# Block sums of two head pairs turned in one product, token rows stored ahead of their gate weights, and seven steps at other places of a hand-written order

## The chip, the core and the metric

The kernel runs on one core of one Trainium2 chip. The engines named here are TensorE (PE; its weight loads are PEld in the trace), VectorE (DVE), ScalarE (ACT), GpSimd (POOL) and SyncE (SP, which issues most transfers). The metric is the device time of one execution in microseconds, as the median of several runs.

## The reference

Local-plus-summary attention, and a mixture of experts on its output, cut to what matters:

```python
k_sum = k.reshape(B, H, nb, block, D).max(axis=3)      # B=2, H=8, S=768, D=64, block=32, nb=24
v_sum = v.reshape(B, H, nb, block, D).mean(axis=3)
scores_all = concat([where(|i-j| < 16, scale*q@k.T, -1e9), scale*q@k_sum.T + log(block)])
x = (softmax(scores_all) @ concat([v, v_sum])).reshape(1536, 512)
logits = x @ w_gate;  expert = argmax(logits);  gate_w = max softmax(logits)     # 8 experts
h = relu(x_of_expert @ w1[e]);  y = h @ w2[e];  out[token] = gate_w * y          # capacity 384
```

## The kernel before, in words

**Attention.** Two heads are worked on together; there are eight such pairs c = 0 to 7, four per batch. Each pair has three groups of four query tiles, so 24 groups n. A group has five steps, whose names stand in the order list: S (scores, PE, L284), M (row maxima, DVE, L291), E (exponentials, four ACT instructions, L295), R (turn, four PE transposes, L299) and K (copy of the turned block, ACT, L304). `V` with a pair and a half (V00, V01, ..., V71) is the product with the values (PE, L310), `N` its normalization (DVE, two steps, L321). Scores lie in two PSUM buffers that alternate (in the first half of the list in three), probabilities in two, so S of a group waits for E of two groups before.

**Keys and values of a pair.** `k`, `q`, `t`, `v` with a number are the loads (SP). `w` copies key windows, `kb` takes block maxima on DVE, `kp` copies them behind the windows (its letter p, v or a is the engine: POOL, DVE or ACT). `vb` sums the values over blocks on DVE into `vsq` (L262), `vt` turns these sums with one PE transpose into a corner of the PSUM tile `bank` (L266), `vk` copies the corner to `vrow` (ACT, L269), `vp` and `vP` copy `vrow` under the value windows (POOL, L272). `bank` also holds the gate logits and the token lists, and a PE product into it waits for an ACT copy out of it that stands ahead in the order list.

**Routing.** For each batch r, `x` turns token rows (PE), `X` copies them, `l`/`L`/`g` make the gate logits, `ch` chooses experts, `pf` makes prefix sums, `pl` places tokens (its last steps write `colm`, L430), `ga` makes the gate weight and stores the rows of the batch to `xrow` in DRAM (L443). `tk0` (PE, L459) makes the token lists of batch 0, `rows` (DVE) the row numbers of the first expert's tokens, `fr0` to `fr2` (POOL) fetch those rows indirectly.

**Experts.** Three rounds, their names without a letter, with B and with C. `lw`/`lW` load w1 and w2 in four parts, `h1g` rounds part g of w1 (or `h2g` of w2) to its high part, `s1g` (and `s2g`) takes the low part as a difference; a letter at the end is the engine (`s10v`: low part of w1, part 0, on DVE, L584). `T`, `H`, `I` turn a third of the fetched rows (PE), round it (ACT) and take its low part `xl` (DVE). `u0` to `u7` are the up products (PE, L629: high by high, low by high, high by low), `D` the down products (L646).

**What sets the order.** The list `SEQ` (L113) is written by hand; each name in it records its instructions at once, and every engine executes its own instructions in that order. An instruction at the head of its engine's row that waits holds all behind it. SP's transfers go through one hardware queue, and each also waits for an earlier use of one of eight completion semaphores.

Of the kernel before, what the change touches and what calls it, by code (L numbers as in the profile page):

```python
# [110 lines left out]


SEQ = """  # L113
q1 k1 t0 S0 k2 t2 S1 M0 E0 M1 Q11a q2 Q10p w1p q3 kb1 S2 E1 kp1v R0 M2 S3 E2 vb0 R1 z2 z3 t1 K0 K1 k3 v0 Q20p w2p vt0 M3 kb2 v2 vk0 S4 vb2 kp2p E3 v1
R2 Q21a M4 S5 q4 K2 t3 E4 Q30p vP0 k4 R3 M5 Q31a vp0 S6 vb1 E5 misc t4 R4 M6 w3p q6 S7 K3 kb3 v3 E6 vt1 M7 V00 kp3p q5 vk1 K4 V01 vp1 N00 N00 vP1 R5
N01 N01 E7 S8 K5 R6 M8 S9 K6 E8 R7 M9 vt2 vk2 V10 E9 vP2 V11 N10 N10 Q41a Q40p S10 N11 N11 K7 vp2 k5 vb3 R8 S11 M10 t5 K8 w4p kb4 E10 R9 M11 vt3 kp4p
V20 vk3 K9 vP3 V21 N20 E11 vb4 S12 vp3 N21 t6 N20 Q60p k6 Q61a N21 R10 M12 k7 R11 K10 S13 E12 vt4 K11 M13 V30 vk4 V31 E13 Q50p N30 N30 S14 N31 Q51a
N31 w5p kb5 R12 x0 M14 K12 kp5p x1 vb5 X0a x2 X1a S15 t7 vb6 X2a q7 E14 v6 vt5 M15 l00 w6p vk5 kb6 v5 R13 L00a E15 R14 w7p v4 kb7 x3 g00 K13 v7 S16
X3a kp6p vb7 K14 vP4 x4 M16 x5 Q70p X4a S17 X5a vp4 Q71a vt6 kp7p E16 M17 l01 vp5 R15 vP5 L01a E17 S18 vk6 g01 K15 M18 vp6 R16 ch0 S19 vP6 E18 ch0 ch0
ch0 ch0 R17 ch0 ch0 M19 S20 ch0 ga0 E19 ga0 ga0 pf0 ga0 pick pick pick M20 pick pick pick pick first lw0 lw1 lw2 lw3 V40 pl0 K16 pl0 V41 N40 pl0 K17  # L120
N40 S21 N41 N41 pl0 pl0 pl0 R18 pl0 pl0 E20 R19 vt7 vk7 vP7 vp7 zr V50 pl0 pl0 pl0 pl0 K18 M21 V51 K19 N50 N50 E21 tk0 rows rows S22 N51 N51 ts0 pads
pads R20 pads M22 rows fr0 S23 K20 pads E22 pads pads pads firstB R21 fr1 M23 K21 V60 E23 V61 fr2 N60 N60 h10a R22 N61 N61 R23 K22 s10v V70 K23 V71
lW0 lW1 lwB0 h11p h12p h13p N70 N70 x6 x7 X6a x8 X7v N71 N71 T0 X8a T1 H0 l10 I0 H1 I1 L10a T2 x9 H2 x10 I2 g10 X9v X10a x11 u0 X11a s11v l11 L11a
# [12 lines left out]
def attention_moe(ctx: ExitStack, tc: tile.TileContext, qT, kT, vT, vw, wg, w1, w2, cf, cm, cr, cv, out, cap: int):  # L136
    nc = tc.nc
# [12 lines left out]
    xrow = dram.tile([N, XW], F32, name="xrow")  # L150
# [179 lines left out]
    class Route:  # L330
# [22 lines left out]
        def take(self, i, eng):  # L353
            self.xt[i] = work.tile([P, KD, P], F32, tag="xt", name="xt", bufs=LB)
            cast(eng, self.xt[i], self.xp[i])

        def logits(self, j):
            self.lq[j] = psum.tile([P, LB, P], F32, tag="x" if self.n == 0 else f"av{j}", name="lq", bufs=1)
            for i in range(LB):
                for kk in range(KD):  # L360
                    nc.tensor.matmul(self.lq[j][32 * kk : 32 * kk + 32, i, :], wgt[:, kk, :], self.xt[LB * j + i][:, kk, :], start=True, stop=True)

        def logits_keep(self, j, eng):
            self.lqs[j] = work.tile([P, LB, P], F32, tag="lqs", name="lqs", bufs=1)
# [82 lines left out]

    def clip(cn, name):
# [525 lines left out]
```

## Time and profile before

| what | value |
|---|---|
| median of 3 runs (lowest, highest) | 188.87 us (188.63, 191.33) |
| the profiled execution's own time | 189.09 us |
| its span, first to last instruction | 187.0 us |
| what lies around the span | 2.09 us |
| PE busy, PEld busy | 174.2 us (93%), 156.2 us (84%) |
| DVE, ACT, POOL busy | 104.7, 101.3, 67.3 us |
| mean granted TensorE clock | 0.992 |

The span falls into two parts. Up to about 75 us attention and routing run, with all engines at work; from there to about 180 us the three expert rounds run, and PE works through nearly without a gap. A busy PE row counts matmuls that overlap, so gaps are read from the weight loads (PEld): idle time ahead of one, and what ended it, is a real stop of PE. A row of the timeline is start, duration, engine, line, operation, output and inputs, shapes, count, and in brackets the idle time before it and what ended that.

### The profile page before, as it was taken

The numbers are of one execution on the slowest core, as the hardware profiler recorded it, in microseconds if no ns is written. First come the engines' busy times: TensorE is split into PE (matmuls) and PEld (weight loads), VectorE is DVE, ScalarE is ACT, GpSimd is POOL, SyncE is SP. The second block draws the span as 40 slices with busy tenths as digits, with TensorE's granted clock in tenths as the row PEclk, the third lists the DMA queues.
The fourth block names the chain that finished last, engine by engine and source line by source line (L and its number), as shares of the span: only waits on it lengthen the run. The fifth ranks groups of instructions, "written<-read, shape, count | busy, mean of one in ns | idle before, by whom it ended". The sixth has DMA issues, their size and how long they took to land. (4 is left out here: it accounts for less than half of the span.)

```text
span 187.0 us, 3978 instructions
## 1 busy us (share of the span) xinstructions
PE 174.2 (93%) x1461; PEld 156.2 (84%) x1461; DVE 104.7 (56%) x226; ACT 101.3 (54%) x223; POOL 67.3 (36%) x84
## 2 busy tenths in 40 slices
PE   6969999999898979999999999999999999999950
PEld 2858899999698968999987889999888999988830
DVE  3499668695389876469998476455611932210000
ACT  4679999998875757346455375445324722211110
POOL 7399758566614599200072341200022110002220
PEclk9999999999999999999999999999999999999996
DMA  6989999939949995277999999970011010001011
GB/s 188 332 318 307 272 365 312 378 93 295 270 147 285 354 404 176 81 255 266 259 407 319 351 389 401 413 294 4 0 56 55 1 60 0 2 4 56 29 38 58
DMA packets 20375, 38.77 MB, mean 207 GB/s; under 512 B 1482, under 2 KB 8572, under 8 KB 20348
## 3 DMA queue, kind: packets, MB, share of 16 engines
q1 hardware_dynamic: 18416, 33.43, 54.2%
q0 software_dynamic: 1440, 4.73, 6.3%
q10 hardware_dynamic: 492, 0.28, 0.6%
q8 instruction: 13, 0.21, 0.5%
q14 instruction: 14, 0.11, 0.2%
HBM read 29.77 MB, written 8.66 MB: 206 GB/s over the span
## 5 line engine op out<-in xcount | busy, mean ns | idle before, releaser
L646 PE MATMUL yp<-w,h 128*128 128x512 f32 x216 | 50.4, 391 | 0.0
L646 PEld LDWEIGHTS yp<-w,h 128*128 128x128 f32 x216 | 40.3, 188 | 8.2
L629 PE MATMUL hp<-xh,w1h 128*128 128x384 f32 x96 | 32.8, 341 | 0.0
L629 PE MATMUL hp<-xh,w1l 128*128 128x384 f32 x96 | 32.2, 335 | 0.0
L629 PE MATMUL hp<-xl,w1h 128*128 128x384 f32 x96 | 32.1, 335 | 0.0
L659 POOL DMA_INDIRECT out<-y,oid x9 | 9.7, 1081 | 60.8 <-ACT y L656 57.5
L297 ACT ACTIVATE prob<-sc,nm 128x120 f32<-128x120 f32 x96 | 27.0, 371 | 6.6 <-DVE nm L293 2.7
L288 PE MATMUL sc<-k,qb 128*128 128x120 f32 x192 | 26.7, 283 | 2.3 <-DVE k L236 1.8
L288 PEld LDWEIGHTS sc<-k,qb 128*128 128x128 f32 x192 | 24.0, 196 | 3.7 <-POOL k L230 2.4
L634 ACT ACTIVATE h<-hp 128x384 fp32r<-128x384 f32 x24 | 11.8, 492 | 27.6 <-PE hp L629 27.6
L638 DVE SCALAR_TENSOR_TENSOR h<-hp,h 128x384 fp32r<-128x384 f32 x24 | 13.3, 555 | 21.1 <-ACT h L634 21.1
L293 DVE TENSOR_REDUCE nm<-sc 128x4 f32<-128x480 f32 x24 | 15.7, 653 | 10.7 <-PE sc L289 8.6
L656 ACT ACTIVATE y<-yp,xgb 128x512 f32<-128x512 f32 x9 | 6.2, 688 | 28.5 <-PE yp L646 18.9
L230 POOL TENSOR_SCALAR v<-vrow 25x1040 f32<-25x1040 f32 (+1 forms) x16 | 13.8, 860 | 12.6 <-ACT vrow L270 11.8
L629 PEld LDWEIGHTS hp<-xh,w1h 128*128 128x128 f32 x96 | 18.0, 188 | 0.3 <-issue 0.2
L629 PEld LDWEIGHTS hp<-xl,w1h 128*128 128x128 f32 x96 | 18.0, 188 | 0.1
L629 PEld LDWEIGHTS hp<-xh,w1l 128*128 128x128 f32 x96 | 18.0, 188 | 0.0
L590 DVE TENSOR_TENSOR w<-w2r,w 128x1024 fp32r<-128x1024 f32 x12 | 14.6, 1222 | 6.1 <-ACT w L234 5.4
L584 DVE TENSOR_TENSOR w1l<-w1r,w1h 128x1024 fp32r<-128x1024 f32 x10 | 13.1, 1320 | 3.0 <-ACT w1h L234 2.8
L302 PE MATMUL pt<-cft,prob 128*121 128x128 f32 x96 | 14.8, 282 | 0.0
L306 ACT COPY pts<-pt 121x512 f32<-121x512 f32 x24 | 13.8, 603 | 1.6 <-PE pt L302 1.2
L234 ACT CAST w<-w2r 128x1024 fp32r<-128x1024 f32 x12 | 12.6, 1050 | 3.1 <-PE yp L646 2.5
(125 smaller groups left out, 229.7 us busy)
## 6 DMA issues: line engine op xcount, KB each, us to landing
w1r<-w SPq DMA_DIRECT2D x12, 512.0 KB, 8.3
w2r<-w SPq DMA_DIRECT2D x12, 512.0 KB, 6.3
v<-vw SPq DMA_DIRECT2D x16, 292.5 KB, 7.3
kc<-kT SPq DMA_DIRECT2D x8, 400.0 KB, 6.3
xrow<-x SPq DMA_DIRECT2D x2, 1542.0 KB
vc<-vT SPq DMA_DIRECT2D x8, 384.0 KB, 6.1
out<-zrow SPq DMA_DIRECT2D x2, 1536.0 KB
qc<-qT SPq DMA_DIRECT2D x7, 384.0 KB, 6.3
```

Source lines behind the costliest of these rows:

```text
L230: eng.tensor_scalar(out=dst, in0=src, scalar1=f, scalar2=0.0, op0=ALU.mult, op1=ALU.add)
L234: nc.scalar.copy(out, in_)
L288: nc.tensor.matmul(self.sc[:, i, :], qb[c % NQ][:, t, :], kt[c][:, t, :], start=i == 0, stop=False)
L293: nc.vector.tensor_reduce(out=self.nm, in_=self.sc, op=ALU.max, axis=AX.X, negate=True)
L297: nc.scalar.activation(self.pr[:, i, :KW], self.sc[:, i], AF.Exp, bias=self.nm[:, i : i + 1])
L302: nc.tensor.transpose(self.pt[:KV, P * i : P * i + P], self.pr[:, i], ident)
L306: nc.scalar.copy(self.pts[:KV], self.pt[:KV])
L584: eng.tensor_tensor(out=self.w1l[g], in0=self.w1r[g], in1=self.w1h[g].bitcast(F32), op=ALU.subtract)
L590: eng.tensor_tensor(out=self.w2[g][:, 1], in0=self.w2r[g], in1=self.w2[g][:, 0].bitcast(F32), op=ALU.subtract)
L629: nc.tensor.matmul(ps, a[g][:, kk, fo : fo + P], x[:, kk, :], start=n == 0, stop=n == 3 * KD - 1)
L638: nc.vector.scalar_tensor_tensor(out=h[:, f % 2, 1], in0=self.hp[f], scalar=0.0, in1=h[:, f % 2, 0].bitcast(F32), op0=ALU.max, op1=ALU.sub ...
L646: nc.tensor.matmul(ps, self.h[g][:, i, a, P * j : P * j + P], self.w2[g][:, w, i, :], start=n == 0, stop=n == 3 * KF - 1)
```

## The change

- Block sums of values: pairs 0 and 2, pairs 4 and 5, and pairs 6 and 7 put their sums side by side into one `vsq` (24 columns at 96, 24 at 64), and one transpose turns both. Pairs 1 and 3 stay alone. `vt2`, `vt5` and `vt7` are gone from the list; the eight copies `vk` stay, two behind each shared turn. `vrow` has three buffers, and the third gets its constant rows by one more small transfer (`vr`, SP).
- Rows of a batch are stored in two transfers: 512 columns ahead (`xw0` between the loads `v4` and `v7`; `xw1` behind `N71`), and the two columns with token number and gate weight (8 bytes per row, 768 pieces) where the whole store stood.
- Steps at other places: `kp1` from DVE to ACT, ahead of `E1`; `vt0`/`vk0` and `vk2` into the stretch of `S5` to `E5`; `vt4 vk4 vk5` behind `l00`; `vk6 vk7` ahead of `L01a`; `S22` and `M22` ahead of `tk0` and `rows`; `h10a` from behind `N60` to behind `K23`; `s10v` and `lwB0` from behind `K22` to behind `I1`.

```diff
+PAIRS = (0, 2), (1,), (3,), (4, 5), (6, 7)
-... N60 N60 h10a R22 N61 N61 R23 K22 s10v V70 K23 V71 lW0 lW1 lwB0 ... N71 N71 T0 X8a T1 H0 l10 I0 H1 I1 L10a T2
+... N60 N60 R22 N61 N61 R23 K22 V70 K23 h10a V71 lW0 lW1 ... N71 N71 xw1 T0 X8a T1 H0 l10 I0 H1 I1 s10v lwB0 L10a T2
     def value_blocks(c):
-        vsum[c] = vsq[c % 2]
-        nc.vector.tensor_reduce(out=vsum[c][:, WIN:KW], in_=vc[c].rearrange("p (n j) -> p n j", j=BLK), op=ALU.add, axis=AX.X)
+        p, i = next((p, x.index(c)) for p, x in enumerate(PAIRS) if c in x)
+        vsum[c], at[c] = vsq[p % 2], WIN - BLK * i
+        nc.vector.tensor_reduce(out=vsum[c][:, at[c] : at[c] + NB], in_=vc[c].rearrange("p (n j) -> p n j", j=BLK), op=ALU.add, axis=AX.X)
     def value_blocks_keep(c):
-        nc.scalar.copy(vrow[c % 2][WIN:KW, :, :D], vtrn[WIN:KW].rearrange("p (h d) -> p h d", d=D))
+        nc.scalar.copy(vrow[c % 3][WIN:KW, :, :D], vtrn[at[c] : at[c] + NB].rearrange("p (h d) -> p h d", d=D))
             nc.vector.reciprocal(out=X[self.b][:, self.u0 : self.u0 + self.T, DM + 1], in_=sm)
             yield
-            nc.sync.dma_start(
-                out=xrow[P * self.t0 : P * (self.t0 + self.T)].rearrange("(i p) d -> p i d", p=P), in_=X[self.b][:, self.u0 : self.u0 + self.T, :],
-            )
+            self.write(DM, XW)
+        def write(self, lo=0, hi=DM):
+            rows = xrow[P * self.t0 : P * (self.t0 + self.T)].rearrange("(i p) d -> p i d", p=P)
+            nc.sync.dma_start(out=rows[:, :, lo:hi], in_=X[self.b][:, self.u0 : self.u0 + self.T, lo:hi])
+    def last_vrow():
+        nc.sync.dma_start(out=vrow[2][WIN:KV], in_=cv)
+        op(f"xw{r}", rt.write)
```

PE's row at the turn of pair 1's sums (`vsq1`), just ahead of V00, with the engines each row waits for; `sc` are the scores of group 7, `pts` the copied blocks of group 0. Before:

```order
L289 LDWEIGHTS cmt_76
L289 MATMUL sc_331<-cmt_76 128x4x96
L267 MATMUL bank_93<-cft_75,vsq1_86 128x128 [waits DVE_49]
L316 MATMUL av_351<-v0_234,pts_228 64x65 [waits DMAHW1_49,Pool_49]
L316 MATMUL av_351<-v0_234,pts_228 64x65 x7
```

After:

```order
L291 LDWEIGHTS cmt_76
L291 MATMUL sc_334<-cmt_76 128x4x96
L269 MATMUL bank_94<-cft_75,vsq1_86 128x128 [waits DVE_49,Activation_49]
L318 MATMUL av_354<-v0_236,pts_230 64x65 [waits DMAHW2_49,Pool_49]
L318 MATMUL av_354<-v0_236,pts_230 64x65 x7
```

The turn now waits for ACT too: the copy `vk2` reads the same corner of `bank` and stands on ACT behind E5.

ACT's row at the end of routing's logits of batch 0: `lqs` is L01a, `prob0` and `prob1` are E16 and E17, `vrow` are copies of turned sums (vk6, and after the change vk6 and vk7). Before:

```order
L297 ACTIVATE prob0_83<-sc_769,nm_787 128x120 x4
L234 COPY lqs_835<-lq_815 128x384
L297 ACTIVATE prob1_84<-sc_797,nm_813 128x120 x4
L270 COPY vrow0_87<-bank_93 24x2x64
L306 COPY pts_851<-pt_829 121x512
```

After:

```order
L299 ACTIVATE prob0_83<-sc_770,nm_788 128x120 x4
L272 COPY vrow0_87<-bank_94 24x2x64
L272 COPY vrow1_88<-bank_94 24x2x64
L235 COPY lqs_838<-lq_816 128x384
L299 ACTIVATE prob1_84<-sc_798,nm_814 128x120 x4
L308 COPY pts_853<-pt_830 121x512
```

Both copies stand ahead of `lqs` now, where one stood behind E17 and the other came in the stretch of E20.

DVE's row at the start of the experts: `rz` and `x1` are the normalizations N61, N70 and N71, `xt` is X7v, `xl` are I0, I1 and I2, `w1l0` is s10v. Before:

```order
L327 TENSOR_TENSOR x1_99<-av_1162,rz_1188 128x3x128
L584 TENSOR_TENSOR w1l0_1198<-w1r0_941,w1h0_1181 128x1024
L324 RECIPROCAL rz_1239<-av_1200 128x6
L327 TENSOR_TENSOR x1_99<-av_1200,rz_1239 128x3x128
L236 COPY xt_1259<-xp_1247 128x512
L324 RECIPROCAL rz_1261<-av_1215 128x6
L327 TENSOR_TENSOR x1_99<-av_1215,rz_1261 128x3x128
L611 TENSOR_TENSOR xl_1291<-xgp_1264,xh_1276 128x4x128
L611 TENSOR_TENSOR xl_1291<-xgp_1271,xh_1276 128x4x128
L611 TENSOR_TENSOR xl_1291<-xgp_1297,xh_1276 128x4x128
```

After:

```order
L329 TENSOR_TENSOR x1_100<-av_1162,rz_1186 128x3x128
L326 RECIPROCAL rz_1236<-av_1196 128x6
L329 TENSOR_TENSOR x1_100<-av_1196,rz_1236 128x3x128
L237 COPY xt_1256<-xp_1244 128x512
L326 RECIPROCAL rz_1258<-av_1213 128x6
L329 TENSOR_TENSOR x1_100<-av_1213,rz_1258 128x3x128
L615 TENSOR_TENSOR xl_1289<-xgp_1262,xh_1274 128x4x128
L615 TENSOR_TENSOR xl_1289<-xgp_1269,xh_1274 128x4x128
L588 TENSOR_TENSOR w1l0_1293<-w1r0_943,w1h0_1211 128x1024
L615 TENSOR_TENSOR xl_1289<-xgp_1298,xh_1274 128x4x128
```

The low part of w1's first quarter moves from ahead of N70 to between I1 and I2.

## Rows read from the trace of the kernel before

**Rows 1.** Busy time by stretch, late in the expert rounds (PE, PEld, DVE, ACT, POOL)

```profile
150.00:160.00 10.00, 10.00 (x59) 10.00 (x58) 2.69 (x6) 2.26 (x5) 0.36 (x1) 1.00 0.07 28
```

**Rows 2.** Timeline, weight loads with idle time ahead, whole span

```profile
11.55 0.97 PEld L288 LDWEIGHTS sc<-k,qb 128*128 128x128 f32 x8 [1.96 <-POOL k L230]
16.58 0.97 PEld L288 LDWEIGHTS sc<-k,qb 128*128 128x128 f32 x8 [0.39 <-POOL k L230]
...
50.26 0.74 PEld L369 LDWEIGHTS bank<-cft,lqs 128*128 128x128 f32 x6 [0.67 <-ACT vrow L270]
...
60.13 0.54 PEld L459 LDWEIGHTS <-rowm 128*128 128x128 bf16 x12 [0.62 <-DVE colm L430]
67.77 1.04 PEld L316 LDWEIGHTS av<-v,pts 121*64 121x64 f32 x32 [0.57 <-ACT pts L306]
70.11 0.97 PEld L350 LDWEIGHTS xp<-cft,x 128*128 128x128 f32 x9 [0.93 <-DVE x L327]
...
100.23 0.42 PEld L603 LDWEIGHTS xgp<-cft,xgb 128*128 128x128 f32 x4 [0.24 <-DMA xgb<-xrow,bids]
```

**Rows 3.** Timeline, start of the kernel: kp1v on DVE

```profile
10.15 1.28 DVE L236 COPY k<-ks 128x288 f32<-128x288 f32 x1
```

**Rows 4.** Timeline: E5 on ACT, turns of pairs 1 and 2 on PE

```profile
19.11 1.12 ACT L297 ACTIVATE prob<-sc,nm 128x120 f32<-128x120 f32 x4
19.37 0.14 PEld L267 LDWEIGHTS bank<-cft,vsq 128*128 128x128 f32 x1
```

**Rows 5.** Timeline, routing of batch 0: ACT, POOL, DVE, then batch 1's colm

```profile
48.41 0.50 ACT L234 COPY lqs<-lq 128x384 f32<-128x384 f32 x1
49.95 0.26 ACT L270 COPY vrow<-bank 24x128 f32<-24x128 f32 x1
58.74 2.04 POOL L230 TENSOR_SCALAR v<-vrow 25x1040 f32<-25x1040 f32 x2 [6.69 <-ACT vrow L270]
58.92 1.37 DVE L430 TENSOR_TENSOR colm<-kt,eqj 128x144 bf16<-128x144 bf16 x2
87.21 0.52 DVE L430 TENSOR_TENSOR colm<-kt,eqj 128x144 bf16<-128x144 bf16 x2
```

**Rows 6.** Timeline: E21 on ACT, M22 on DVE, S23 on PE

```profile
60.96 1.12 ACT L297 ACTIVATE prob<-sc,nm 128x120 f32<-128x120 f32 x4 [1.20 <-DVE rz L324]
62.12 0.97 PEld L288 LDWEIGHTS sc<-k,qb 128*128 128x128 f32 x8
62.94 0.65 DVE L293 TENSOR_REDUCE nm<-sc 128x4 f32<-128x480 f32 x1
```

**Rows 7.** Timeline, from the store of batch 0's rows to the first up product

```profile
54.11 0.40 SPq L443 DMA_DIRECT2D xrow<-x  x1
61.68 0.18 DVE L496 TENSOR_REDUCE aids<-apk 128x3 int32<-128x24 f32 x1
63.34 1.21 POOL L575 DMA_INDIRECT xgb<-xrow,aids  x1 [1.97 <-PE sc L288]
67.25 4.04 POOL L230 TENSOR_SCALAR w1h<-w1r 128x1024 fp32r<-128x1024 f32 x3
67.26 2.10 DVE L584 TENSOR_TENSOR w1l<-w1r,w1h 128x1024 fp32r<-128x1024 f32 x1 [0.99 <-ACT w1h L234]
71.25 4.70 POOL L584 TENSOR_TENSOR w1l<-w1r,w1h 128x1024 fp32r<-128x1024 f32 x2
72.46 1.29 DVE L611 TENSOR_TENSOR xl<-xgp,xh 128x512 fp32r<-128x512 f32 x2 [0.15 <-ACT xh L607]
75.72 1.31 DVE L584 TENSOR_TENSOR w1l<-w1r,w1h 128x1024 fp32r<-128x1024 f32 x1
75.81 0.34 PE L629 MATMUL hp<-xl,w1h 128*128 128x384 f32 x1
```

**Rows 8.** Landing of the nine row fetches; page: ACT's queue (packets, MB, share)

```profile
DMA to landing us min/median/max: 4.6/6.5/7.2
q10 hardware_dynamic: 492, 0.28, 0.6%
```

More of the change, by code (lines that the diff above doesn't have):

```diff
@@ L113 @@
 SEQ = """
[L114 to L121, printed above, removed]
@@ L122 @@
-pads R20 pads M22 rows fr0 S23 K20 pads E22 pads pads pads firstB R21 fr1 M23 K21 V60 E23 V61 fr2 N60 N60 h10a R22 N61 N61 R23 K22 s10v V70 K23 V71
-lW0 lW1 lwB0 h11p h12p h13p N70 N70 x6 x7 X6a x8 X7v N71 N71 T0 X8a T1 H0 l10 I0 H1 I1 L10a T2 x9 H2 x10 I2 g10 X9v X10a x11 u0 X11a s11v l11 L11a
+q1 k1 t0 S0 k2 t2 S1 M0 E0 M1 Q11a q2 Q10p w1p q3 vr kb1 kp1a S2 E1 R0 M2 S3 E2 vb0 R1 z2 z3 t1 K0 K1 k3 v0 Q20p w2p M3 kb2 v2 S4 vb2 kp2p E3 v1 R2
+Q21a M4 S5 vt0 q4 K2 vk0 t3 E4 Q30p vP0 k4 R3 M5 Q31a vp0 S6 vb1 E5 vk2 misc t4 R4 M6 w3p q6 S7 K3 kb3 v3 E6 vt1 M7 V00 kp3p q5 vk1 K4 V01 vp1 N00 N00
@@ new lines @@
+vP1 R5 N01 N01 E7 S8 K5 R6 M8 S9 K6 E8 R7 M9 V10 E9 vP2 V11 N10 N10 Q41a Q40p S10 N11 N11 K7 vp2 k5 vb3 R8 S11 M10 t5 K8 w4p kb4 E10 R9 M11 vt3 kp4p
+V20 vk3 K9 vP3 V21 N20 E11 vb4 S12 vp3 N21 t6 N20 Q60p k6 Q61a N21 R10 M12 k7 R11 K10 S13 E12 K11 M13 V30 V31 E13 Q50p N30 N30 S14 N31 Q51a N31 w5p
+kb5 R12 x0 M14 K12 kp5p x1 vb5 X0a x2 X1a S15 t7 vb6 X2a q7 E14 v6 M15 l00 w6p vt4 vk4 vk5 kb6 v5 R13 L00a E15 R14 w7p v4 xw0 kb7 x3 g00 K13 v7 S16
+X3a kp6p vb7 K14 vP4 x4 M16 x5 Q70p X4a S17 X5a vp4 Q71a vt6 kp7p E16 M17 l01 vp5 R15 vP5 vk6 vk7 L01a E17 S18 g01 K15 M18 vp6 R16 ch0 S19 vP6 E18 ch0
@@ new lines @@
+ch0 ch0 ch0 R17 ch0 ch0 M19 S20 ch0 ga0 E19 ga0 ga0 pf0 ga0 pick pick pick M20 pick pick pick pick first lw0 lw1 lw2 lw3 V40 pl0 K16 pl0 V41 N40 pl0
+K17 N40 S21 N41 N41 pl0 pl0 pl0 R18 pl0 pl0 E20 R19 vP7 vp7 zr V50 pl0 pl0 pl0 pl0 K18 M21 V51 K19 N50 N50 E21 S22 tk0 M22 rows rows N51 N51 ts0 pads
+pads R20 pads rows fr0 S23 K20 pads E22 pads pads pads firstB R21 fr1 M23 K21 V60 E23 V61 fr2 N60 N60 R22 N61 N61 R23 K22 V70 K23 h10a V71 lW0 lW1
+h11p h12p h13p N70 N70 x6 x7 X6a x8 X7v N71 N71 xw1 T0 X8a T1 H0 l10 I0 H1 I1 s10v lwB0 L10a T2 x9 H2 x10 I2 g10 X9v X10a x11 u0 X11a s11v l11 L11a
@@ L160, in attention_moe @@
     vsq = [const.tile([P, P], F32, name=f"vsq{i}") for i in range(2)]
-    vrow = [const.tile([P, 2, D + 1], F32, name=f"vrow{i}") for i in range(2)]
+    vrow = [const.tile([P, 2, D + 1], F32, name=f"vrow{i}") for i in range(3)]
     soh = [const.tile([P, E], BF16, name=f"soh{i}") for i in range(4)]
@@ L250, in queries @@
         scaled(eng, dst, src, 0.125)
-    ksum, vsum = {}, {}
+    ksum, vsum, at = {}, {}, {}
     vtrn = corner(P)[:, 0]
@@ L269, in value_blocks_keep @@
     def value_blocks_keep(c):
-        nc.scalar.copy(vrow[c % 2][WIN:KW, :, :D], vtrn[WIN:KW].rearrange("p (h d) -> p h d", d=D))
+        nc.scalar.copy(vrow[c % 3][WIN:KW, :, :D], vtrn[at[c] : at[c] + NB].rearrange("p (h d) -> p h d", d=D))
     def value_blocks_put(c, t0, t1):
-        src = vrow[c % 2][WIN:KV].rearrange("p h d -> p (h d)").unsqueeze(1).to_broadcast([KV - WIN, t1 - t0, 2 * (D + 1)])
+        src = vrow[c % 3][WIN:KV].rearrange("p h d -> p (h d)").unsqueeze(1).to_broadcast([KV - WIN, t1 - t0, 2 * (D + 1)])
         scaled(nc.gpsimd, vt[c][WIN:KV, t0:t1].rearrange("p t h d -> p t (h d)"), src, 1.0)
@@ L880, in attention_moe @@
         op(f"pf{r}", rt.prefix)
+        op(f"xw{r}", rt.write)
         chain(f"pl{r}", rt.place)
         chain(f"ga{r}", rt.gate)
-    for name, f in dict(misc=misc, zr=zeros, nr=count, set=settle, tk0=census, tk1=last_census, ts0=first_tokens, ts1=all_tokens, cl1=last_clip).items():
+    for name, f in dict(misc=misc, vr=last_vrow, zr=zeros, nr=count, set=settle, tk0=census, tk1=last_census, ts0=first_tokens, ts1=all_tokens, cl1=last_clip).items():
         op(name, f)
```

## The prediction, made before the run

> **What bounds the kernel now.** I read three views in turn. First the busy time by stretch: late in the expert rounds PE is busy for all of a stretch of 10 us, while DVE, ACT and POOL have 2.69, 2.26 and 0.36 us of work in it [rows 1]. The DMA share there is 0.07. So from about 75 us on nothing but PE sets the time, and the change leaves PE's work there as it is. Second the timeline of the weight loads, where each idle time is a real stop of PE [rows 2]. Ahead of 76 us those that the change touches are 1.96 and 0.39 (a key copy), 0.67 (a copy out of `bank`), 0.62 (`colm`), 0.57 (a copied block) and 0.93 us (a normalization). Behind 76 us one matters, 0.24 us for batch 1's fetched rows. Third the timeline of the other engines from the store of batch 0's rows to the second up product, `hp<-xl`, at 75.81 us [rows 7]. It needs the rows fetched, turned, rounded and their low parts taken, and behind it PE is never again short of work but for the 0.24. **So the gain is the time by which that product starts earlier, and at most 0.24 us more.** Two us off the path of PE in the middle of attention are worth nothing by themselves if the fetch does not start earlier.
>
> **The front, up to 48 us.** `kp1` took 1.28 us on DVE [rows 3]; on ACT, where a copy of 128x384 took 0.50 us [rows 5], I estimate 0.4 by its 288 columns. The scores that stopped for 1.96 us can start up to 0.85 us earlier. But the next key copy, POOL's, stopped PE for 0.39 us [rows 2] and has not moved, so no more than 0.39 of it is kept, and ACT does 0.4 us more ahead of E1. I take 0.1, from 0 to 0.39. Against it stands a new wait: the turn of pair 1's sums ran at 19.37 us; now it waits for `vk2`, which stands on ACT behind E5, and E5 ran from 19.11 for 1.12 us [rows 4]. With a copy of 0.26 us [rows 5] that ends at 20.49, so PE stops for at most 1.12 us, and V00 and all of PE's row with it. E5 itself should come a little earlier, and vt0's own turn is out of the way; I take 0.5, from 0 to 1.12. Two turns of 0.14 us [rows 4] fall away here (`vt2`; `vt4` and `vt5` become one): 0.28 back. The sum is 0.1 - 0.5 + 0.28, about 0.1 us lost, with bounds of 0.8 lost and 0.7 gained.
>
> **Routing, 48 to 62 us.** `g01` stopped for 0.67 us until a copy from 49.95 us for 0.26 had ended [rows 2, 5]. Now both copies stand ahead of `L01a`, which started at 48.41; 48.41 + 2 x 0.26 + 0.50 gives 49.43, so `g01` goes at about 49.65, when PE has come that far, in place of 50.26: 0.6 gained, of at most 0.67. The list of steps of DVE that makes the tokens' places starts 0.5 us earlier (0.6 less 0.1). Its last two, `colm`, took 1.37 us in batch 0 beside POOL's copies under the value windows, and 0.52 us in batch 1 with POOL free [rows 5]. These copies waited 6.69 us for pair 7's `vk7`, which is early now, so POOL makes them by 53 or so: 0.85 gained (from 0). PE's `tk0` is reached sooner, but the end of E21 (60.96 + 1.12 = 62.08) held the next scores at 62.12 [rows 6]. What E21 waited for, a normalization, comes earlier with PE. Together PE is 0.5 + 0.14 (the third dropped turn) + about 0.5 (of the 0.62 [rows 2], since S22 now fills it) = 1.15 us early.
>
> **The fetch.** The row numbers ended at 61.68 + 0.18 = 61.86 us [rows 7]. They gain 0.5 + 0.85 and lose M22, 0.65 us [rows 6], which now stands ahead of them on DVE, whatever part of it doesn't fit into DVE's wait for `tk0`: they end at about 61.2. POOL's first fetch started at 63.34, not at 61.86. The page names PE, but PE's work was done; the fetch also waits for the store of the rows, issued at 54.11, and I take that as the late one. The store's 512 columns now go out while attention still runs, and only 768 pieces of 8 bytes are left: 48 for each of the 16 DMA engines. A small piece of ACT's queue took 0.6% of 16 engines' 187 us over 492 packets, 36 ns [rows 8]; 48 of them are 1.8 us behind the loads ahead of them, so they should be there before the row numbers. I take **F = 61.6 us** for the first fetch, from 61.2 to 63.34; 1.74 us gained.
>
> The Trainium skill speaks against this split: "DMA: Bandwidth & Descriptors", section "Specifications", asks for transfers of at least 512 bytes for the full rate and says that below it the DMA engine reads, modifies and writes. No row of before shows an 8-byte store, so by that page it could end as late as the whole store did, and the sum would lose the 1.74 us.
>
> **From the fetch to the second up product.** PE has, besides the 1.15, the stops of 0.57 and 0.93 us to win [rows 2]: `h10a` stood on ACT ahead of a block copy that V70 needs, and `s10v` on DVE ahead of N70, which X6 needs. Both have moved behind what was held. So PE can turn the first third 2.65 us earlier, but the fetched rows (6.5 us from issue to landing [rows 8]) are 1.74 us earlier. I0 and I1 ended at 72.46 + 1.29 = 73.75 [rows 7], and will end by 72.0, perhaps 71.1. Next on DVE is now `s10v`, and then I2, which the second up product waits for (I2 is the last third of `xl`).
>
> What `s10v` costs there is the heart of it. In before it took 2.10 us, started at the same time as the first of POOL's three casts, and those took 4.04 [rows 7]. If one of the two holds the other off, cast and low part c and a follow from c + a = 2.11 (67.25 to 69.36) and 3c + a = 4.04: c = 0.97, a = 1.15 us. Alone-standing figures agree: `s11v` took 1.31 us beside the very end of POOL's work [rows 7]. I therefore read the row as: whichever starts second waits until the first instruction has ended. POOL's casts started at 67.25, 3.91 us behind the fetch; after the change they start at F + 3.91 = 65.5, take 3 x 0.97 = 2.9 as no `s10v` stands between, and its two low parts of 2.35 each follow (4.70 for two [rows 7]): 68.4 to 70.75 and 70.75 to 73.1. `s10v`, ready at 71.1 to 72.0, finds the second begun, waits to 73.1 and ends at 74.25. I2, half of 1.29, ends at 74.9, and the second up product starts at about 75.0 in place of 75.81: **0.8 us gained**. In general this is F + 13.4.
>
> The Trainium skill names this: "SBUF — State Buffer", section "SBUF: two separate sides", says that VectorE and GpSimd share a port pair as an exclusive lock which the first to start holds for its whole instruction, a VectorE instruction with two SBUF inputs included. The 2.10 us agree with it; without that rule `s10v` would cost its own time alone, which is rival A.
>
> **Batch 1.** Its rows are stored early too, and its fetch was the 0.24 us stop [rows 2]: 0.24 gained. One product more or less of a turn, and the small load for the third `vrow`, cost nothing that PE waits for: SP's queue has them beside loads, and if that cover were gone a load of a key would be late by the issue, 0.40 us [rows 7].
>
> **Sum.** 189.09 (the profiled execution: span and 2.09 around it) - 0.8 - 0.24 = 188.05; the median stands 0.22 below the profiled one, which gives 187.8. Since the front's bounds lie more on the losing side than on the other, I say **188.0 us**.
>
> **Rivals.** *A: `s10v` is not held.* Either it and POOL share, or it is ready before POOL's second low part starts and takes the gap (71.1 against 70.75: a tie of 0.35 us). Then it ends by 73.2 at the latest (72.0 + 1.15), I2 at 73.8, or with the gap at about 72.5 and PE's own turns set I2. The product starts at 73.1 to 73.9, 1.9 to 2.7 us early, and the time is 186.0 to 186.8. For it speaks the tie; against it the 2.10 us. Chance 0.22.
> *B, the other side: the fetch starts no earlier.* The 8-byte pieces land as late as the whole store, or the wait was for something else that hasn't moved. Then F = 63.34, the product starts at 63.34 + 13.4 = 76.75, 0.95 us late because `s10v` now stands ahead of I2 behind POOL's low part: 188.87 + 0.95 - 0.24 = 189.6. It decides from F = 62.65 on. For it speaks that the store was issued 9.2 us ahead of the fetch and would have been late all the same, with loads around it; against it that only 8 bytes of each row are left. Chance 0.18.
> *C: the change does little.* The dropped turns are worth 3 x 0.14 us, and one of them stood ahead of a wait; the new wait at `vk2` takes its full 1.12, and routing starts no earlier. Then F is near 62.3 and the time 188.4 to 188.9. Chance 0.10.
>
> **How the numbers follow.** The forecast has 0.50 and its own range is 187.3 to 188.4. The range of 186.2 to 189.3 adds most of A, all of C and the mild half of B (F up to 63). A measurement of this kernel can tell about 2%, 3.8 us; no case here reaches it, since all stops that the change can remove ahead of 76 us come to 5.1 us and most are held by the next wait. So faster by over 2% has 0.04, slower 0.02, within 0.94.
>
> **What would show it.** In the profile of the changed kernel: the turn of pair 1's sums stops for about 0.5 us on ACT's `vrow`; no stop ahead of `g01` for `vrow`; `colm` near 0.5 us; the first fetch at 61.2 to 62; no stops of 0.57 and 0.93; `s10v` well over 1.2 us, ending about 1.1 us behind POOL's last low part; the second up product near 75.0, 0.8 us ahead of before. If `s10v` takes 1.2 us and the product starts at 73 to 74, A was right; if the fetch starts behind 62.65, B. A span that moves differently from that product would show that PE is not all that bounds the rounds.

## The result, and the profile after

| | before | changed |
|---|---|---|
| median of 12 runs, beside each other | 189.2 us (187.83 to 191.33) | 190.52 us (189.09 to 191.67) |
| ratio, 95% interval | 1 | 1.0061 (1.0036 to 1.0087) |
| profiled execution, its span | 189.09, 187.0 us | 190.60, 188.5 us |
| second up product starts | 75.81 us | 77.33 us |
| from there to the end of the span | 111.19 us | 111.17 us |
| mean granted TensorE clock | 0.992 | 0.982 |

The changed kernel is slower by 0.6%, where 0.5% faster was forecast, and 190.52 us lies above the range (186.2 to 189.3). By 2% it is no change; with 12 runs each the sign is clear on this chip. The time behind the second up product is the same to 0.02 us, so all of the 1.5 us came about ahead of it. The comparisons here and below leave disturbed executions out; the profiled ones of e9 and e12 are of that kind.

These are the weight loads of the changed kernel with idle time ahead (start, duration, engine, line, operation, shapes, count, idle time and what ended it), answering to [rows 2]:

```profile
11.02 0.97 PEld L290 LDWEIGHTS sc<-k,qb 128*128 128x128 f32 x8 [0.95 <-POOL k L231]
16.84 0.97 PEld L290 LDWEIGHTS sc<-k,qb 128*128 128x128 f32 x8 [1.18 <-POOL k L231]
20.16 0.14 PEld L269 LDWEIGHTS bank<-cft,vsq 128*128 128x128 f32 x1 [0.84 <-ACT vrow L272]
...
43.25 0.42 PEld L352 LDWEIGHTS xp<-cft,x 128*128 128x128 f32 x4 [0.51 <-ACT lqs L235]
...
49.30 0.97 PEld L290 LDWEIGHTS sc<-k,qb 128*128 128x128 f32 x8 [0.42 <-POOL v L231]
...
70.23 0.42 PEld L607 LDWEIGHTS xgp<-cft,xgb 128*128 128x128 f32 x4 [1.58 <-ACT xt L235]
71.73 0.42 PEld L607 LDWEIGHTS xgp<-cft,xgb 128*128 128x128 f32 x4 [1.08 <-issue]
```

The stops of 0.67, 0.62, 0.57 and 0.93 are gone, as forecast. In their place stand 0.84 at vt1, 0.51 at x3, and 1.58 and 1.08 at T0 and T1; the latter two are waits for fetched rows (the matmuls' rows behind them name the transfer of `xgb`). The same stretch by the other engines, answering to [rows 5, 7]:

```profile
49.60 3.58 POOL L231 TENSOR_SCALAR v<-vrow 25x520 f32<-25x520 f32 x4 [0.62 <-ACT vrow L272]
51.79 0.76 DVE L383 TENSOR_TENSOR val<-val,cft 128x48 f32<-128x48 f32 x1
52.82 0.42 DVE L387 TENSOR_TENSOR oh<-val,m 128x48 bf16<-128x48 f32 x1
59.16 0.52 DVE L432 TENSOR_TENSOR colm<-kt,eqj 128x144 bf16<-128x144 bf16 x2
61.77 0.18 DVE L500 TENSOR_REDUCE aids<-apk 128x3 int32<-128x24 f32 x1
62.84 1.21 POOL L579 DMA_INDIRECT xgb<-xrow,aids  x1 [9.07 <-PE sc L291]
69.80 4.66 POOL L588 TENSOR_TENSOR w1l<-w1r,w1h 128x1024 fp32r<-128x1024 f32 x2
73.65 1.88 DVE L588 TENSOR_TENSOR w1l<-w1r,w1h 128x1024 fp32r<-128x1024 f32 x1
75.51 0.69 DVE L615 TENSOR_TENSOR xl<-xgp,xh 128x512 fp32r<-128x512 f32 x1
77.33 0.33 PE L633 MATMUL hp<-xl,w1h 128*128 128x384 f32 x1
```

The first fetch starts at 62.84, not 61.6; s10v is held for 1.88 us, up to 1.07 us behind POOL's last low part (69.80 + 4.66 = 74.46), as forecast. And here is what no part of the prediction had, busy time by stretch (the last three columns are granted clock, DMA share and GB/s):

```profile
71.00:72.00 1.00, 0.24 (x2) 0.27 (x3) 0.45 (x1) 0.51 (x1) 1.00 (x1) 1.00 0.99 385
72.00:73.00 1.00, 1.00 (x20) 0.82 (x22) 0.24 (x1) 0.57 (x1) 1.00 (x2) 0.70 1.02 377
73.00:74.00 1.00, 1.00 (x17) 0.61 (x10) 0.95 (x2) 0.15 (x2) 1.00 (x1) 0.50 1.05 373
74.00:75.00 1.00, 1.00 (x6) 1.00 (x6) 1.00 (x1) 0.45 (x2) 0.45 (x1) 0.50 0.97 342
75.00:76.00 1.00, 1.00 (x8) 1.00 (x7) 1.00 (x2) 0.47 (x1) 0.00 (x0) 0.59 0.22 68
```

After the two stops TensorE's clock is granted at half, 1.2 of 2.4 GHz, from about 72.4 to 75.8 us. The 24 small products of l10 took 1.49 us there, 0.86 in before. So PE's own row set the start of the up products, and not I2, which had ended at 76.20:

```profile
72.32 1.49 PE L363 MATMUL lq<-xt,wgt 128*32 128x128 f32 x24
```

### The profile page after: what moved, and what is told of

It is laid out like the page before. It is cut to its first block, busy times and chain, and to the rows that moved or that the text cites. A ratio compares the mean times of both kernels' runs of the same rounds, so it can differ in the third digit from the quotient of the medians.

```text
span 188.5 us, 3980 instructions
## 1 busy us (share of the span) xinstructions
PE 175.0 (93%) x1458; PEld 157.3 (83%) x1458; DVE 103.0 (55%) x225; ACT 101.5 (54%) x224; POOL 66.1 (35%) x84
## 5 line engine op out<-in xcount | busy, mean ns | idle before, releaser
L231 POOL TENSOR_SCALAR v<-vrow 25x1040 f32<-25x1040 f32 (+1 forms) x16 | 13.4, 841 | 2.6 <-ACT vrow L272 0.9
L304 PE MATMUL pt<-cft,prob 128*121 128x128 f32 x96 | 14.2, 277 | 0.0
```

Of the source, the lines that this page charges most:

```text
L231: eng.tensor_scalar(out=dst, in0=src, scalar1=f, scalar2=0.0, op0=ALU.mult, op1=ALU.add)
L304: nc.tensor.transpose(self.pt[:KV, P * i : P * i + P], self.pr[:, i], ident)
```

## The experiments

All comparisons are with the kernel before on the same chip; F is the start of the first fetch and U that of the second up product in the one profiled execution, and the last column counts executions with a mean granted clock up to 0.985 over the whole execution, wherever in it the clock fell. "Held" says whether PE's weight loads in that trace stop several times between 62.5 and 69 us for nothing that the profile names; this went by the chip, not by the kernel.

| kernel | held | ratio, 95% interval | F | U | U - F | clock low |
|---|---|---|---|---|---|---|
| before | no | 1 | 63.34 | 75.81 | 12.47 | - |
| changed | no | 1.0061 (1.0036 to 1.0087) | 62.84 | 77.33 | 14.49 | 5 of 12 |
| e1: stops filled | yes | 1.0011 (0.9980 to 1.0043) | 62.16 | 76.07 | 13.91 | 0 of 12 |
| e2: no 8-byte store | yes | 0.9993 (0.9959 to 1.0028) | 62.46 | 75.81 | 13.35 | 0 of 12 |
| e3: s10v behind N70 | yes | 0.9983 (0.9949 to 1.0017) | 63.26 | 75.95 | 12.69 | 2 of 12 |
| e4: one store | yes | 1.0036 (1.0002 to 1.0070) | 63.66 | 77.29 | 13.63 | 4 of 12 |
| e5: changed again | no | 1.0041 (1.0009 to 1.0073) | 62.24 | 76.37 | 14.13 | 7 of 12 |
| e6: tk0 first | no | 1.0012 (0.9980 to 1.0044) | 61.55 | 74.91 | 13.36 | 0 of 12 |
| e7: mended | no | 0.9890 (0.9829 to 0.9950) | 61.69 | 74.52 | 12.83 | 0 of 6 |
| e8: before, split alone | no | 0.9983 (0.9948 to 1.0019) | 62.63 | 75.09 | 12.46 | 1 of 12 |
| e9: tk0 first, s10v behind N70 | yes | 1.0085 (1.0042 to 1.0128) | 61.35 | 78.57 | 17.22 | 4 of 7 |
| e10: copies mended | yes | 0.9969 (0.9938 to 1.0000) | 62.52 | 75.89 | 13.37 | 1 of 12 |
| e11: before, moves alone | yes | 1.0002 (0.9967 to 1.0038) | 63.70 | 77.07 | 13.37 | 1 of 12 |
| e12: mended, again | yes | 1.0017 (0.9980 to 1.0053) | 62.12 | 78.70 | 16.58 | 5 of 12 |
| e13: mended, s10v as before | no | 0.9931 (0.9898 to 0.9965) | 62.74 | 75.28 | 12.54 | 2 of 12 |
| e14: changed again | no | 1.0023 (0.9987 to 1.0058) | 62.01 | 75.37 | 13.36 | 2 of 12 |
| e15: h10a, s10v as before | no | 0.9974 (0.9937 to 1.0011) | 62.93 | 75.31 | 12.38 | 2 of 12 |
| e16: tk0 first, again | no | 1.0007 (0.9968 to 1.0047) | 63.18 | 76.55 | 13.37 | 1 of 12 |
| e17: stops filled, again | yes | 1.0009 (0.9975 to 1.0042) | 63.79 | 77.61 | 13.82 | 0 of 12 |
| e18: changed, beside e17 | yes | 0.9991 (0.9957 to 1.0024) | 63.07 | 76.46 | 13.39 | 0 of 12 |

The three theories at first were: the loss is the clock (1), it is I2 behind a held s10v (2), or it is the fetch (3).

**The stops filled (e1, e17).** Ten turns of the identity ahead of T0, six ahead of T1:

```diff
-N71 N71 xw1 T0 X8a T1
+N71 N71 xw1 wm0 T0 X8a wm1 T1
+    def keep_busy(n):
+        for _ in range(n):
+            nc.tensor.transpose(vtrn, ident, ident)
```

> The changed kernel with 16 turns of the identity more on PE (ten ahead of T0, six ahead of T1; each took 0.14 us of weight load), which fill the two stops of 1.58 and 1.08 us that PE has there while it waits for the fetched rows; their product is read by nobody. Theory 1 (the loss is TensorE's clock, which the profile shows at 1.2 GHz from 72.3 to 75.6 us, right behind these stops): the clock stays at 2.4 GHz, l10 to x11 run at the durations of before, and the second up product starts about 1 us earlier than 77.33 (it still waits for I2); time 189.0 to 189.6. Rival theory 2 (the loss is I2, held behind s10v on DVE): the clock is as in the changed kernel or not, the second up product stays near 77.3, and the time near 190.5.

> The changed kernel with 16 turns of the identity more on PE (ten ahead of T0, six ahead of T1), as in the first run, now beside the unaltered one. Theory: a clock below 0.986 in 0 to 2 of 12 executions, where the unaltered one has it in 2 to 7; the second up product 13.4 to 13.9 us behind the first fetch; time up to 0.3% below the unaltered one. If the clock falls as often, the stops at T0 and T1 are not its cause.

The clock fell in none of 24 executions. But on both chips PE was held at 64 to 67 us and came late to T0 anyway, and the unaltered kernel beside e17 has no fall either, so these runs don't show that filling the stops is the cure. The turns cost something there: U - F is 13.8 to 13.9 in place of 13.4.

**The changed kernel again (e5, e14, e18).**

> The changed kernel once more, unaltered, for another profiled execution and for a comparison on the chip on which the next three run. What is seen again is the kernel's, what is not is one execution's. Theory: the row numbers end at about 61.9 us with the first fetch 0.88 us behind them, s10v is over 1.2 us long, and PE stands at T0 and T1; the ratio to the kernel before is near 1.006.

> The changed kernel, unaltered, on the chip of the other three. If PE is held at 64 to 67 us on this chip, PE arrives late at T0, the two stops there are short, the clock holds in more executions than on the other chips (where it fell in about half), and the ratio is nearer 1.00 than 1.006. If PE isn't held there: as before, 1.004 to 1.006.

> The changed kernel, unaltered, on the same chip as the one with the stops filled. Theory: the clock falls in 2 to 7 of 12 executions; where the profiled execution shows the fall, the second up product is more than 14 us behind the first fetch, and 13.4 where it doesn't; ratio to the kernel before 1.002 to 1.006.

In four sets of runs the unaltered kernel gives 1.0061, 1.0041, 1.0023 and 0.9991, with the clock low in 5, 7, 2 and 0 of 12. In the first three traces PE isn't held, in the fourth it is. Without a fall U - F is 13.36 and 13.39 (e14, e18), with one 14.49 and 14.13 (the first and e5): the fall cost 1.1 and 0.8 us in those two executions. e14 had stops of 1.39 and 0.90 without a fall:

```profile
69.20 0.42 PEld L608 LDWEIGHTS xgp<-cft,xgb 128*128 128x128 f32 x4 [1.39 <-ACT xt L236]
70.52 0.42 PEld L608 LDWEIGHTS xgp<-cft,xgb 128*128 128x128 f32 x4 [0.90 <-issue]
75.36 0.19 PEld L634 LDWEIGHTS hp<-xl,w1h 128*128 128x128 f32 x1 [0.95 <-DVE xl L616]
```

e5 fell with stops of 1.48 and 0.80, no longer in sum. So the same program falls in some executions and not in others, with stops of much the same length. In the last row PE waits 0.95 us for I2 behind s10v: with the clock up, theory 2 holds.

**The small store (e2), and one store (e4).** In e2 the early store of batch 0 takes all columns, with the gate weight's set to 1 where the token numbers are written; e4 has neither xw0 nor xw1.

```diff
+        nc.gpsimd.memset(X[0][:, :, DM + 1], 1.0)
...
-            self.write(DM, XW)
+            if self.b:
+                self.write(DM, XW)
...
-        op(f"xw{r}", rt.write)
+        op(f"xw{r}", rt.write, 0, DM if r else XW)
```

> The changed kernel without the second, 8-byte store of batch 0: the token numbers and a constant 1 in place of the gate weight go out with the early store, so batch 0's tokens are not weighted by their gate. It asks what held the first fetch at 62.84 us, 0.89 us behind its row numbers (61.95). If it was the small store's landing: the fetch starts about 0.3 us behind the row numbers, as batch 1's fetch does in the changed kernel (91.01 to 91.28), so at about 62.2, and PE's stops ahead of T0 and T1 shrink by 0.6 in all. If it was something else (PE's products or the loads), the fetch stays near 62.8. Time: 189.9 by the first, 190.5 by the second.

> The changed kernel with each batch's rows stored in one transfer at the old place (no xw0, xw1); all else as changed. If the split brought the earlier fetch: the fetch starts at 63.3 or later as in the kernel before, T0 stops longer than 1.58 us, the clock falls all the more, and batch 1's fetch goes back from 91.3 to about 93.7 + 1.5 with a stop at TB0; time 190.8 to 191.5. If the early store of batch 1's rows at 69.9 us, which fills the DMA engines from 70 to 76, is what makes the fetched rows late (7.3 us to landing against 6.8): T1 and T2 stop less, the clock may hold, and the time falls below 190.

Without the 8-byte store the fetch still starts 0.89 us behind the row numbers (61.57 to 62.46). In e4, with whole stores, it was 1.83 us behind (61.83 to 63.66). So the split did what it is for, and the small store isn't late. A delay of 0.88 to 0.90 is in every trace but those of before and e4; batch 1's fetch, whose last wait is on the fetch itself and not on an instruction ahead of it, was 0.27 us behind its row numbers (91.01 to 91.28). The fetched rows landed 6.9 us behind their issue in e4 (median), 7.3 in the changed kernel's first trace and 6.9 in e14's: the early store of batch 1's rows isn't shown to delay them.

**The split alone, in the kernel before (e8).**

```diff
-... v4 kb7 ... N71 N71 T0
+... v4 xw0 kb7 ... N71 N71 xw1 T0
```

> The kernel before with the split store alone (512 columns early, 8 bytes per row at the old place). If the whole store's landing held the first fetch in the kernel before (1.48 us behind the row numbers at 61.86): the fetch starts 0.9 us behind the row numbers, at about 62.7, and batch 1's at about 90 instead of 93.7 with no stop at TB0; the rest as before; time 0.3 to 0.6 us below the kernel before. If the 8-byte pieces or the early store of batch 1's rows (which fills the DMA engines from 70 us on) cost more than that: same or slower.

```profile
62.63 1.21 POOL L577 DMA_INDIRECT xgb<-xrow,aids  x1 [1.38 <-DVE mine L778]
75.09 0.34 PE L631 MATMUL hp<-xl,w1h 128*128 128x384 f32 x1
```

The fetch is 0.88 us behind the row numbers and U 0.72 us earlier than before in this execution, of which 0.59 came between the scores of group 18 and the fetch (14.15 us for 14.74); the ratio leaves it open (0.9983). The whole store isn't late each time: in e11, which has it, the fetch was 0.88 us behind. And the stop ahead of TB0 is gone, but the time from U to TB0's product is 24.45 us, before 24.44: it was no stop of PE.

**tk0 ahead of S22 again (e6, e16).**

```diff
-E21 S22 tk0 M22 rows rows N51 N51 ts0 pads pads R20 pads rows fr0
+E21 tk0 rows rows S22 N51 N51 ts0 pads pads R20 pads M22 rows fr0
```

> The changed kernel with one of its seven steps undone: tk0 and the row numbers stand ahead of S22 and M22 again, as in the kernel before. Theory 3 (the early S22 holds tk0 on PE for 0.97 us, and so eats what colm gains): tk0 starts right behind colm's end, the row numbers and the first fetch come 0.8 to 0.9 us earlier (61.0 and 61.9 us), the fetched rows too; PE stands less at T0 and T1; time 0.4 to 0.8 us below the changed kernel. Rival: PE's lost time at tk0 (0.6 us, as in the kernel before) is passed on, T0 is set by PE, and nothing is gained.

> The changed kernel with tk0 ahead of S22 once more, beside the unaltered one on the same chip. Theory: the fetch 0.7 to 0.9 us earlier than in the unaltered one, the time 0.3 to 0.6% lower. If the first result was the chip's: no difference.

Counted from the start of S18 (the scores of group 18 on PE: 49.30 us in the changed kernel, 48.70 in e5, 48.60 before and in e6), the fetch comes 13.54 us later in the changed kernel and in e5, 12.95 in e6 and 12.83 in e16. So the two steps moved ahead cost the fetch 0.6 to 0.7 us. Theory 3 blames S22 on PE; the rows of DVE say that it was M22 (`nm`), which stands ahead of the row numbers (`apk`, then `aids`). In e5:

```profile
59.80 0.56 DVE L330 TENSOR_TENSOR x<-av,rz 128x384 f32<-128x384 f32 x1
60.39 0.66 DVE L296 TENSOR_REDUCE nm<-sc 128x4 f32<-128x480 f32 x1
60.97 0.17 DVE L494 TENSOR_TENSOR apk<-bank,eq 128x24 f32<-128x24 f32 x1
```

In e6, on the same chip:

```profile
59.80 0.56 DVE L329 TENSOR_TENSOR x<-av,rz 128x384 f32<-128x384 f32 x1
60.28 0.17 DVE L493 TENSOR_TENSOR apk<-bank,eq 128x24 f32<-128x24 f32 x1
```

The profile names no idle time of DVE in either, and up to `x` both are alike to 0.01 us. The product tk0 had ended on PE ahead of `apk` both times (60.57 and 59.57), so it held nothing. No run has S22 ahead and M22 behind; by these times I estimate that `apk` would then wait for tk0 until 60.57, 0.3 us at most.

The ratio fell by 0.3% (e5 to e6) and 0.15% (e14 to e16); no interval is that narrow, though the clock was low in 1 of 24 executions where it had been in 9 of 24.

**s10v at other places (e3, e9, e11, e15).** e3 puts it behind N70, e9 that and tk0 first; e11 makes the changed kernel's two moves in the kernel before; e15 takes them back in the changed one:

```diff
-N60 N60 R22 ... K22 V70 K23 h10a V71 lW0 lW1 ... I1 s10v lwB0 L10a
+N60 N60 h10a R22 ... K22 s10v V70 K23 V71 lW0 lW1 lwB0 ... I1 L10a
```

> The changed kernel with s10v (and the load lwB0) on DVE behind N70 instead of behind I1. Theory 2 (I2 late behind a held s10v): s10v is done by about 70 us, I2 follows H2 at once, and the second up product starts earlier by about 0.7 us at either clock; time 189.6 to 189.9. Theory 1 alone (the clock): PE's stops ahead of T0 and T1 are unchanged or longer, the clock falls as before, and as PE's own products at 1.2 GHz set the start of the up products, the time stays near 190.5.

> The changed kernel with two repairs: tk0 and the row numbers ahead of S22 and M22, and s10v behind N70; its copies of turned sums stay where the change put them. Theory: the first fetch as in the run with tk0 first (61.5 us), the second up product 12.7 to 12.9 us behind it instead of 13.4, so near 74.3; time 0.3 to 0.5 us under that run. If all of the gain of the mended kernel came from the copies, it stays at that run's ratio (1.001).

> The kernel before with h10a behind K23 and s10v and lwB0 behind I1, all else as before. By the prediction's rival B: the fetch stays at 63.3 us, the stops of 0.57 and 0.93 us go, s10v is held by POOL's second low part (near 2 us), and the second up product starts 13.4 us behind the fetch, at 76.7; time 0.9 us above the kernel before, and more where the clock falls. If s10v gets in between POOL's two low parts, or I2 goes ahead, the second up product starts at 75 or sooner, and the time is below the kernel before.

> The changed kernel with only h10a and s10v with lwB0 back at their places of before. Theory: I2 is no longer held (0.7 us), the stops of 0.57 and 0.93 come back ahead of V70 and X6, where they only shorten those at T0 and T1, so that the clock holds; ratio 0.4 to 0.8% below the unaltered one. If the two moves gained what they were meant to gain: slower than the unaltered one by up to 0.5%.

Apart from e1 and e17 with their extra turns, the column U - F sorts the kernels by where s10v stands, as long as the clock holds: 13.35 to 13.39 behind I1 (e2, e6, e10, e11, e14, e16, e18), 12.38 to 12.54 at the place of before (before, e8, e13, e15). The move of h10a and s10v together costs 0.9 us. Behind N70 it is a race with POOL:

```profile
69.06 5.66 POOL L589 TENSOR_TENSOR w1l<-w1r,w1h 128x1024 fp32r<-128x1024 f32 x2
69.39 3.11 DVE L589 TENSOR_TENSOR w1l<-w1r,w1h 128x1024 fp32r<-128x1024 f32 x1
72.42 0.68 DVE L238 COPY xt<-xp 128x512 f32<-128x512 f32 x1
73.16 0.63 PEld L608 LDWEIGHTS xgp<-cft,xgb 128*128 128x128 f32 x4 [2.18 <-DVE xt L238]
```

This is e12, whose s10v stands at the same place. It came 0.33 us behind the start of POOL's first low part, waited it out (3.11 us for an instruction that takes 1.2), the copy X7v behind it was late, T1 stopped for 2.18 us, and the clock fell. In e3, on a held chip too, it started 0.23 us ahead of that low part (69.97 and 70.20) and took 1.33. In e7, on a chip where PE isn't held, DVE was there at 67.27, among POOL's casts, and it took 1.45. e9's execution looks the same, with 3.24 us.

**The copies (e10), and all mended (e7, e12, e13).**

```diff
-vb1 E5 vk2 misc ... v6 M15 l00 w6p vt4 vk4 vk5 kb6 v5 R13 L00a
+vb1 vk2 E5 misc ... v6 vt4 M15 l00 w6p vk4 kb6 v5 R13 L00a vk5
```

> The changed kernel with the copies alone repaired: vk2 ahead of E5, vt4 ahead of l00 with vk5 behind L00a; S22, s10v as changed. Theory: the stop of 0.84 us at vt1 and that of 0.51 at x3 shrink or go, PE and the fetch come up to 0.7 us earlier, but PE then stands the longer at T0, and the clock still falls in about half of the executions; time 0 to 0.5 us under the changed kernel.

> The changed kernel with four repairs: tk0 ahead of S22 as in the run before; s10v behind N70; vk2 ahead of E5 (so that the turn of pair 1's sums doesn't wait 0.84 us for it); vt4 ahead of l00 and vk5 behind L00a (so that L00a isn't 0.75 us later). Theory (each of these steps had cost what the trace of after shows): the stops of 0.84 at vt1 and 0.51 at x3 are gone, the fetch starts at about 61.3, I2 follows H2, and the second up product starts at 74.0 to 75.0; time 187.8 to 188.8 where the kernel before has 189.2. Rival (the fetched rows' landing or the executions' scatter sets it all): within 0.3% of the kernel before.

> The mended kernel once more (tk0 ahead of S22, s10v behind N70, vk2 ahead of E5, vt4 ahead of l00 and vk5 behind L00a), since its first comparison had 6 runs. Theory: ratio to the kernel before 0.985 to 0.995. If its first ratio was the scatter: within 0.3% of the kernel before.

> The changed kernel with the copies repaired (vk2 ahead of E5, vt4 ahead of l00, vk5 behind L00a), tk0 ahead of S22, and h10a and s10v with lwB0 back at their places of before. What is left of the change: the shared turns, the split store, vk6 and vk7 ahead of L01a, kp1 on ACT. Theory: s10v meets POOL's casts (0.97 us each) and never its low parts (2.35 us each), so it takes at most 2.1 us; PE's stops are spread over V70, X6 and T0 instead of two long ones, and the clock holds in nearly all executions; the second up product starts 12.8 us behind the fetch; ratio to the kernel before 0.988 to 0.996. Rival: as the other mended kernel, the clock falls in some executions and the ratio is near 1.

With the copies mended the stops of 0.84 and 0.51 are gone (0.22 for POOL's values and 0.25 for a block copy are left), and from S14 to S18 e10 takes 12.12 us where the changed kernel takes 12.43. Its ratio of 0.9969 (to 1.0000), on a chip of the kind on which the unaltered kernel was even, leaves the gain in time open. e7 and e12 are one kernel, 1.1% faster on one chip (6 runs) and even on another; the race above is the likely reason, but one trace of each doesn't show that. e13 has no such race and is the version that beats both kernels: 0.9931 (0.9898 to 0.9965), beside 1.0023 for the changed one on that chip. It keeps the shared turns, the split store and the early vk6 and vk7.

## Why the prediction was wrong, step by step

The time up to U falls into four parts: up to the scores of group 14 (S14), from there to S18, to the first fetch F, and to U. The rows for S14 and S18 of before, then S14 of the changed kernel:

```profile
36.67 0.97 PEld L288 LDWEIGHTS sc<-k,qb 128*128 128x128 f32 x8
48.60 0.97 PEld L288 LDWEIGHTS sc<-k,qb 128*128 128x128 f32 x8 [0.42 <-issue]
36.87 0.97 PEld L290 LDWEIGHTS sc<-k,qb 128*128 128x128 f32 x8
```

| trace | S14 | S14 to S18 | S18 to F | F to U | S14 to U |
|---|---|---|---|---|---|
| before | 36.67 | 11.93 | 14.74 | 12.47 | 39.14 |
| changed (clock fell) | 36.87 | 12.43 | 13.54 | 14.49 | 40.46 |
| e5: changed (clock fell) | 36.27 | 12.43 | 13.54 | 14.13 | 40.10 |
| e14: changed | 36.04 | 12.43 | 13.54 | 13.36 | 39.33 |
| e18: changed | 37.10 | 12.44 | 13.53 | 13.39 | 39.36 |
| e8: before, split alone | 36.55 | 11.93 | 14.15 | 12.46 | 38.54 |
| e13: mended, s10v as before | 37.79 | 12.11 | 12.84 | 12.54 | 37.49 |

- **What bounds the kernel** was right. Span less U is 111.1 to 111.7 us in every trace but e9's (112.5), so nearly every loss and gain is one of U.
- **Batch 1's 0.24 us** was a misread row. The idle time was one of weight loads beside 512-column down products, which take 391 ns where a load takes 188; their loads always idle, 8.2 us in all in the page's group. U to TB0's product took 24.44 us before and 24.47 after, with the idle gone. So idle time ahead of a weight load is not always a stop of PE.
- **The front** was set at 0.1 us lost; S18 started at 49.30 for 48.60, 0.7 later. Of that 0.50 is the change's: from S14 to S18 all 13 traces with its copies take 12.42 to 12.44 us, the three with the copies of before (before, e8, e11) 11.92 or 11.93. This is a move that was missed: behind l00, the turn of pairs 4 and 5 ran at 41.72, both copies waited for it on ACT, and L00a behind them ran at 42.72 for 41.97, which is the 0.51 at x3. The order list showed it; the prediction looked there only for dropped turns. Up to S14 the traces show no difference: it starts at 36.04 to 37.92 us in the 13 and at 36.55 to 37.63 in the three. The wait at vt1 was sized well (0.84 of a forecast 0.5, up to 1.12), and S3's 0.53 us earlier start was lost again at the next key copy on POOL, which stopped PE for 1.18 where it had been 0.39.
- **Routing**: g01's stop went and `colm` took 0.52, as forecast. POOL's copies didn't vanish, they moved to 49.60 to 53.18, beside the choice of the experts, where two instructions of DVE took 0.76 and 0.42 us for 0.41 and 0.21. Still `colm` ended 10.38 us behind S18 for 11.69 before: 1.31 gained of the 1.45 that the forecast had (0.6 and 0.85).
- **The fetch** is the step that failed: 62.84 for 61.6. From S18 the forecast was 12.9 us (61.6 less 48.7); measured are 13.53 or 13.54 in all ten traces of kernels that leave M22 ahead of the row numbers and store the rows early. The row numbers themselves were forecast well: 12.65 us behind S18 for 12.5, with M22's 0.65 us rightly in the sum. The term that was wrong is the delay from the row numbers to the fetch, 0.4 us (61.2 to 61.6), for which the prediction names no row. It is 0.88 to 0.90 in 18 of the 20 traces; in the other two, before and e4, a whole store held the fetch for 1.48 and 1.83. So in before the store hid the delay, and the split could gain 0.59 us there and not 1.1.
- **s10v** was right: it was held to 1.07 us behind POOL's low part, and F + 13.4 was met to 0.05 us by seven kernels. By it the point from which the change loses is F = 62.4 for U alone. In the four traces of the changed kernel F is 62.84, 62.24, 62.01 and 63.07, on both sides of that point as S14 comes early or late. F = 62.84 means 0.4 us lost, which is rival B's outcome by another cause: the 8-byte store wasn't late. Four uncertain terms stood between the rows and F, each with its bounds, and the range took F up to 63 only.
- **The clock** was missing. The prediction had PE at T0 2.65 us earlier and the rows 1.74, so a stop of a microsecond was in its own numbers, but no price for one. A fall cost 1.1 us in the first trace (F to U 14.49 for 13.36) and 0.8 in e5's. In before the same time was idle in smaller pieces, 0.57, 0.93 and three of 0.17 to 0.29, and the clock held in that execution. That the change makes a fall likelier is not shown: on the three chips on which both were counted, the clock was low in 7 of 12 executions of the changed kernel and 4 of 29 of before, in 2 of 12 and 10 of 35, and in 0 of 12 and 5 of 23.

In sum, from S14 to U without a fall: 0.50 lost to S18, 1.20 gained to F, 0.89 lost to U, about 0.2 us lost where the forecast had 0.8 gained. The missed wait at x3 (0.50) and the delay of the fetch (0.49) are that difference. The first trace's 1.5 us are this 0.2, the 0.2 by which its S14 was later, and the 1.1 of the fall. The profiled execution of e14, the same kernel, took 188.74 us, inside the range of 186.2 to 189.3, but by luck: its S14 came early, at 36.04.

Open is what holds PE at 64 to 67 us on some chips (three of the five on which the experiments ran), and what made up the 1.0061 over all executions. Executions of the changed kernel with a low clock were slower by some 0.2 to 0.5 us in the mean than those without, less than in the two traces; and in the first comparison the seven without took 190.35 us in the mean, where before took 189.25. That is 1.1 us more, without a low clock, and the traces account for only 0.2 of it, or 0.8 for executions of before in which the store doesn't hold the fetch (S18 to F 14.15, as in e8 and e11).

## What to carry to other kernels

A wait that is taken away gives back only what it stood above the next one: the store held the fetch for 1.48 us, but 0.88 of that was there without it, and no row that the prediction read showed it bare. Price a step moved ahead on every engine's row that it touches: S22 filled PE's wait, and M22, moved with it, delayed the row numbers that the fetch needed. A copy that is moved out of the way of one engine's work meets other work where it goes; look there too. And stops that are gathered in one place may cost more than their sum in pieces: ask what idles, how long at a stretch, and what the clock does behind it.

## What the runs showed of the hardware

- DVE's subtraction of two SBUF tiles took 1.2 us alone, 1.8 to 2.3 when it came during POOL's second low part, 3.1 to 3.2 when it came at the start of one of 2.35 us. The Trainium skill, "SBUF — State Buffer", section "SBUF: two separate sides", calls this an exclusive lock held for a whole instruction; these durations agree.
- TensorE went to 1.2 GHz behind stops of 1.58 and 1.08 us and back at 75.8 us; the same program with stops of 1.39 and 0.90 kept 2.4 GHz.
- An indirect fetch started 0.88 us behind the last thing it waited for where a separate instruction waited ahead of it, 0.27 where the fetch itself did.
